# One written order for every step up to the second expert layer, in an attention and feed-forward kernel

## The chip, the core and the metric

The kernel runs on one core of a Trainium2 chip. The metric is the device time of one execution in microseconds (us); lower is better. The core has five engines with an instruction stream each: TensorE (PE) multiplies matrices into PSUM, VectorE (DVE) and ScalarE (ACT) do elementwise work and reductions, GpSimd (POOL) does small work here, and SyncE (SP) issues the transfers (DMA).

## What is computed

Inputs are `q`, `k`, `v` of 8 batches × 12 heads × 448 tokens × 64, and two weight matrices of 768×2048 and 2048×768, which the kernel reads as 64-bit numbers.

```python
scores = scale * q @ k.T - log(448);  attn = sigmoid(scores);  x = attn @ v
h = x @ w_in                                  # 3584 x 768 by 768 x 2048
g = where(h > 0, h, exp(min(h, 0)) - 1)
out = g @ w_out                               # 3584 x 2048 by 2048 x 768
```

There is no normalisation over keys: each score has its own sigmoid.

## The kernel before

The work goes batch by batch (b = 0 to 7), and within a batch by pairs of heads (`hp` = 0 to 5; 48 pairs in all). The first batch multiplies 32-bit numbers. Later ones split each 32-bit operand into a high and a low 16-bit part (`split`, L138: ACT makes the high part, L139, and DVE the low part, L140) and multiply three combinations of them, with scales that are powers of two.

A pair is **prepared**: greatest magnitudes on DVE (`absmax`, L143), summed over partitions on PE (`pr`, L131), made into scales on DVE and POOL; then for b=0 transposed on PE (`pt`, L362) and copied (`early`, L366), and for later batches split (`nat`) and transposed by a DMA (L377). Then come **scores** (`psc`, L408), **sigmoid** on ACT (`sg`, L416), for later pairs the split of the sigmoids (`at`, L454 and L455), **values** (`pav`, L480), and the split of the result into `xh` with its greatest magnitude.

When a batch's six pairs are there, `xh` is rescaled (L519 to L532), and the **first expert layer's product** follows (`moe1`, `ph`, L570: 16 tiles of 18 matmuls), with the exponential on ACT (L582), the rest of the nonlinearity on DVE (L584, L585) and the split into `g`. The **output product** of a batch (`moe2`, `po`, L602: 96 steps of 6 matmuls for an even batch) runs among the attention steps of the next batch.

The **weights** need work of their own, once. Each of the 16 tiles of `w_in` (768 KB) is loaded into a ring of five places (`load_w_in`), turned from 64-bit words into magnitudes by two ACT steps (L156, L160) and one DVE step (L161), summed on PE (`si`, L168), scaled, given its sign (L175), and split into `wi`. The 32 half tiles of `w_out` take the same path (`load_w_out`, `so`), but the scale of a half (`swo`) is there only once all 16 of its tiles have been summed.

What sets the order: from the attention of b=1 on, it is written out in the program (`tc.manual_schedule` holds PE, ACT, DVE and SP to program order). All before that, which is the attention and first layer of b=0 with all of `w_in` and most of `w_out`, is ordered by the framework's scheduler, which works with its own estimates of durations; the lists `W_IN`, `W_LOAD`, `W_OUT` and `W_AHEAD` only say beside which step a weight tile is written down. The staging area of `w_in` and the tile `wo` share one buffer (tag `wo`), as do `early` and `g` (tag `g`).

Of the kernel before, what the change touches and what calls it, by code (L numbers as in the profile page):

```python
# [32 lines left out]

@with_exitstack
def attention_ffn(
# [24 lines left out]
    WHOLE = EXACT * NP + 2  # L60
    SP = 4
    SKEW = 2
    W_IN = [1, 3, 6, 9, 12, 15, 16]
    W_LOAD = [1, 1]
    W_OUT = 4
    W_AHEAD = [6, 2]
# [12 lines left out]
    wi = const.tile([P, 2, NK, DF], F16, name="wi")  # L79

# [9 lines left out]
    stage, w_in_words = [], []  # L90
# [18 lines left out]
    def greatest(dst, mx):  # L109

        dg = sb.tile([P, P], BF16, tag="dg", name="dg")
        nc.vector.tensor_scalar(dg, ident, mx, None, op0=ALU.mult)

        def rest():
            pb = ps.tile([P, 512], F32, tag="pm", name="pb", bufs=3)
            nc.tensor.matmul(pb[:, :P], ones, dg, start=True, stop=True)
            al = sb.tile([P, 1], F32, tag="al", name="al", bufs=2)
            nc.vector.tensor_reduce(al, pb[:, :P], axis=AX.X, op=ALU.max)
            power_of_two(dst, al, XTINY)

        return rest

    def sums_of_rows(dst, mx, parts):

        n = mx.shape[1]

        def rest():
            pb = ps.tile([P, 512], F32, tag="pm", name="pr", bufs=3)
            sums = pb[:, : 4 * n].rearrange("p (n x) -> p n x", x=4)
            for r in parts:  # L130
                nc.tensor.matmul(sums[r], ones[:, r], mx, start=True, stop=True)  # L131
# [4 lines left out]
        return rest  # L136

    def split(hi, lo, src, s):  # L138
        nc.scalar.mul(hi, src, s)  # L139
        nc.vector.scalar_tensor_tensor(lo, src, s, hi, op0=ALU.mult, op1=ALU.subtract)  # L140
# [9 lines left out]
    def magnitudes(t, lo, hi, hl, sums, start, stop):  # L150


        u, h = t.bitcast(U32), hi.bitcast(F32)


        nc.scalar.activation(t, h, AF.Abs, scale=2.0**-112)  # L156


        top = hl.bitcast(U16).rearrange("p a (c t) -> p a c t", t=4)[:, :, :, 1]
        nc.scalar.activation(lo, top, AF.Copy, scale=2.0**-13, bias=2.0**-14 - 0.5)  # L160
        nc.vector.scalar_tensor_tensor(  # L161
            u, u, 3, lo, op0=ALU.logical_shift_left, op1=ALU.bitwise_or
        )

# [23 lines left out]
    def load_w_in(n):  # L188

        src = w_in.rearrange("(c p) f -> p c f", p=P)  # L190
        for _ in range(n):
            f = len(w_in_words)
            if f == 0:

                stage.append(sb.tile([P, WR * 2 + WT, NK * P], F32, tag="wo", name="stage"))
            if f < NF:
                st = stage[0][:, f % WR * 2 : f % WR * 2 + 2]
                st = st.rearrange("p a c -> p (a c)").rearrange("p (c x) -> p c x", c=NK)
                nc.sync.dma_start(st.bitcast(U64), src[:, :, f * P : (f + 1) * P])
                w_in_words.append(words(st))  # L200

    def w_in_tile(f):
        lo, hi, hl = w_in_words[f]
        t = stage[0][:, WR * 2 + f % WT].rearrange("p (c x) -> p c x", c=NK)
        sums = ps.tile([P, 512], F32, tag="pm", name=f"si{f}", bufs=3)
        magnitudes(t, lo, hi, hl, sums[:, :P], True, True)
        sum_magnitude(wp[:, f : f + 1], sums[:, :P])
        nc.vector.reciprocal(wr[:, f : f + 1], wp[:, f : f + 1])
        s = sb.tile([P, 1], F32, tag="sw", name=f"swi{f}", bufs=2)
        nc.gpsimd.tensor_scalar(s, wr[:, f : f + 1], 2.0**WTOP, None, op0=ALU.mult)  # L210
        d = wi[:, :, :, f * P : (f + 1) * P]
        signed(t, hi)
        split(d[:, 0], d[:, 1], t, s)

    def w_in_ratios():
# [4 lines left out]
    def load_w_out(wo):  # L220


        for i in range(NH):
            whole = [
                wo[:, i, f + SKEW].rearrange("p j c -> p (j c)").bitcast(F32)
                for f in range(NF - SKEW)
            ] + [
                sb.tile([P, HM], F32, tag="o", name=f"to{i}_{f}", bufs=OB) for f in range(SKEW)
            ]
            sums = ps.tile([P, 512], F32, tag="pav", name=f"so{i}")  # L230
            loads = []

            def load(f):
                if f >= NF:
                    return
# [14 lines left out]
                loads.append(st)  # L250

            early = W_AHEAD[i]
            for f in range(early):
                load(f)
            for f in range(NF):
                load(f + early)
                lo, hi, hl = words(loads[f])
                t = whole[f].unsqueeze(1)
                magnitudes(t, lo, hi, hl, sums[:, :HM], f == 0, f == NF - 1)
                signed(t, hi)  # L260
                yield
            sum_magnitude(wop[:, i : i + 1], sums[:, :HM])
# [3 lines left out]
            for f in range(NF):  # L266
                split(wo[:, i, f, 0], wo[:, i, f, 1], whole[f], s[:, 1 + f : 2 + f])
                yield


# [4 lines left out]
    def load_qk(b, hp):  # L275
# [3 lines left out]
        for i, src in enumerate((q, k)):  # L279
            for j in range(2):  # L280
                nc.sync.dma_start(  # L281
                    raw[:, i * (NC + 1) :][:, :NC, j],
                    src[b, h0 + j, :SM].rearrange("(p c) d -> p c d", c=NC),
                )
# [36 lines left out]
    def prepare(b, hp, raw, rv, xs):  # L321


        u = f"{b}_{hp}"
        n = 1 if b < EXACT else 3
        mx = sb.tile([P, 15], BF16, tag="mx", name=f"mx{u}", bufs=2)
        groups = mx.rearrange("p (n x) -> p n x", x=5)[:, :n, :4]
        absmax(mx[:, 0:4], rv.rearrange("p (a t) d -> p a (t d)", a=4))
        if n > 1:

            absmax(mx[:, 6 : 2 * NC + 7], raw.rearrange("p t h d -> p t (h d)"))
# [3 lines left out]
        pw = sb.tile([P, n], F32, tag="pw", name=f"pw{u}", bufs=2)  # L335
        apart = b >= EXACT and (hp > 2 or hp == (2 if b == EXACT else 0))
        product = sums_of_rows(pw, groups, rows if apart else [slice(0, P)])

        def scales():
            product()  # L340
            sc = sb.tile([P, n + 3], F32, tag="sc", name=f"sc{u}", bufs=5)
            if b >= EXACT:
# [10 lines left out]
            value_scale(b, hp, pw[:, 0:1], sc[:, n : n + 1], xs)  # L353
            return lambda: transposed(sc)

        def transposed(sc):
            x_scale, s_rest, s_scale = (sc[:, n + i : n + i + 1] for i in range(3))
            if b < EXACT:
                pt = ps.tile([P, 2, 512], F32, tag="psc", name=f"pt{u}", bufs=2)
                pt = pt.rearrange("p a x -> p (a x)")  # L360
                for t in range(2 * NC + 1):
                    nc.tensor.transpose(  # L362
                        pt[:, t * P : (t + 1) * P], raw[:, t].rearrange("p h d -> p (h d)"), ident
                    )
                qk = early[:, hp % 2]
                nc.vector.tensor_copy(qk, pt[:, : 2 * S])  # L366
                return x_scale, 1 / math.sqrt(D), [qk], [rv]
            nat = sb.tile([P, 2, 2 * NC + 1, P], F16, tag="nat", name=f"nat{u}")
            for t, n_t, s in (
                (0, NC, sc[:, 1:2]), (NC, 1, s_rest), (NC + 1, NC, sc[:, 2:3])  # L370
            ):
                split(
                    nat[:, 0, t : t + n_t], nat[:, 1, t : t + n_t],
                    raw[:, t : t + n_t].rearrange("p t h d -> p t (h d)"), s,
                )
            qk = sb.tile([P, 2, 2 * NC + 1, P], F16, tag="qk", name=f"qk{u}", bufs=3)
            nc.sync.dma_start_transpose(  # L377
                qk.rearrange("p i t x -> p (i t) x"), nat.rearrange("p i t x -> p (i t x)")
            )
            parts = [qk[:, i].rearrange("p t x -> p (t x)") for i in range(2)]  # L380

            if b * NP + hp < WHOLE:
                whole = sb.tile([P, 2 * NC + 2, D], F32, tag="vn", name=f"vw{u}", bufs=3)
                return x_scale, s_scale, parts, [load_v(b, hp, whole)]
            vn = sb.tile([P, 2, 2 * NC + 2, D], F16, tag="vn", name=f"vn{u}", bufs=3)
            split(vn[:, 0], vn[:, 1], rv, sc[:, 0:1])
            return x_scale, s_scale, parts, [vn[:, 0], vn[:, 1]]

        return scales

    class Pair:
# [42 lines left out]
        def parts(self, g):  # L434
# [435 lines left out]
```

## Time and profile before

| | us |
|---|---|
| median of three runs | 1201.78 (1201.6 to 1202.27) |
| the profiled execution | 1201.61 |
| its span, first to last instruction | 1199.8 |
| busy: PE, DVE, ACT, POOL | 1148.5, 817.2, 710.1, 95.9 |

A stage table gives the busy time of each engine within a stretch. A timeline row gives start, length, engine, line, operation, output and inputs, the number of instructions merged into it, and in brackets the idle time before it with what ended it. A row of groups gives count, busy us, mean ns of one, then the idle time before them. The letter q behind an engine means its queue (SPq: SyncE's issuing).

### The profile page before, as it was taken

How to read it: one execution, taken by the hardware profiler on the slowest of the kernel's cores; microseconds unless marked ns; L12 is line 12 of the kernel's file. 1: busy time of each engine (PE TensorE's matmuls, PEld its weight loads, DVE VectorE, ACT ScalarE, POOL GpSimd, SP SyncE). 2: the span in 40 equal slices, each digit the busy share in tenths (PEclk: the TensorE clock that was granted, in tenths of full speed). 3: DMA queues.
4: the chain of work that ended last, by engine and by line, in shares of the span. 5: the costliest groups of instructions: out<-in, count | busy, mean ns of one | idle time of the engine just before them, and what ended most of it. 6: DMA issues, size and time to landing. Idle time of an engine off the chain costs nothing.

```text
span 1199.8 us, 24004 instructions
## 1 busy us (share of the span) xinstructions
PE 1148.5 (96%) x9662; PEld 634.7 (53%) x9662; DVE 817.2 (68%) x1730; ACT 710.1 (59%) x1087; POOL 95.9 (8%) x275
## 2 busy tenths in 40 slices
PE   6779976999999999999999999999999999999998
PEld 2224433555566555555566555655566555655565
DVE  4798888877577575876677575976667666864500
ACT  4785796855566447864666446865666446864300
POOL 1011001100011001100011000200011000100000
PEclk9989988999999999999999999999999999999999
DMA  8874634521234130531224221441134212310000
GB/s 220 260 191 96 220 107 114 104 61 41 47 79 95 34 68 20 115 78 40 41 65 96 53 51 37 94 100 40 40 61 93 61 40 47 70 30 8 1 27 27
DMA packets 220687, 92.14 MB, mean 77 GB/s; under 512 B 184224, under 2 KB 216480, under 8 KB 220576
## 3 DMA queue, kind: packets, MB, share of 16 engines
q1 hardware_dynamic: 220576, 90.61, 31.3%
q8 instruction: 75, 1.23, 0.4%
q14 instruction: 36, 0.29, 0.1%
HBM read 60.29 MB, written 11.01 MB: 59 GB/s over the span
## 4 chain that ended last, share of the span: by engine, by line
PE 85%; DMA 5%; DVE 4%; ACT 3%; SPq 2%; issue 1%; DVEq 0%; POOL 0%; ACTq 0%; POOLq 0%
PE ph L570 32%; PE po L602 31%; PE pav L480 7%; PE psc L408 7%; PE po_r L602 5%; DMA stage<-in_moe_w_in_dram 3%; PE pscr L500 1%; DMA wo<-in_moe_w_out_dram 1%; SPq L281 1%; ACT sg L416 1%; DMA so<-in_moe_w_out_dram 1%; ACT wo L139 1%; DVE wo L175 1%; DVE wo L140 1%; DVE wi L140 1%
## 5 line engine op out<-in xcount | busy, mean ns | idle before, releaser
L570 PE MATMUL ph<-xh,wi 128*128 128x448 f16 x2304 | 441.7, 353 | 1.7 <-DVE e L585 0.9
L602 PE MATMUL po<-wo,g 128*64 128x384 f16 (+1 forms) x4320 | 395.7, 328 | 6.9 <-ACT wo L139 3.8
L602 PEld LDWEIGHTS <-g 128*64 128x64 f16 (+1 forms) x4992 | 290.3, 109 | 169.6 <-issue 40.4
L570 PEld LDWEIGHTS <-wi 128*128 128x128 f16 x2304 | 223.0, 98 | 214.3 <-issue 8.0
L582 ACT ACTIVATE e<-ph,msc 128x448 f32<-128x448 f32 x128 | 80.7, 631 | 185.8 <-PE ph L570 161.1
L455 DVE SCALAR_TENSOR_TENSOR at<-sg,at 128x896 f16<-128x896 f32 x120 | 127.6, 1091 | 92.2 <-ACT at L454 92.2
L416 ACT ACTIVATE sg<-psc,bias,sc 128x896 f32<-128x896 f32 x126 | 133.5, 1094 | 3.6
L584 DVE TENSOR_SCALAR e<-e 128x448 f32<-128x448 f32 x128 | 50.2, 393 | 117.1 <-ACT e L582 117.1
L454 ACT ACTIVATE at<-sg 128x896 f16<-128x896 f32 x120 | 109.4, 947 | 0.6
L139 ACT ACTIVATE g<-e,msc 128x384 f16<-128x384 f32 (+1 forms) x192 | 96.1, 533 | 11.3 <-DVE e L585 9.9
L139 ACT ACTIVATE xh<-pav,sc 128x448 f16<-128x448 f32 x48 | 30.3, 631 | 119.8 <-PE pav L480 117.3
L140 DVE SCALAR_TENSOR_TENSOR g<-e,msc,g 128x384 f16<-128x384 f32 (+1 forms) x192 | 94.8, 522 | 1.9 <-ACT g L139 1.5
L585 DVE SCALAR_TENSOR_TENSOR e<-ph,msc,e 128x448 f32<-128x448 f32 x128 | 87.5, 684 | 4.1
L408 PE MATMUL psc<-qk 64*128 64x448 f16 x756 | 86.5, 352 | 2.2 <-ACT sg L416 2.2
L480 PE MATMUL pav<-at,vn 128*64 128x448 f16 x720 | 74.8, 353 | 0.0
L139 ACT ACTIVATE nat<-raw,sc 128x384 f16<-128x384 f32 (+1 forms) x126 | 60.7, 535 | 10.2 <-POOL sc L347 8.4
L480 PEld LDWEIGHTS <-vn 128*64 128x64 f16 x880 | 49.9, 110 | 31.2
L349 POOL TENSOR_SCALAR sc<-pw 128x1 f32<-128x1 f32 x42 | 12.2, 292 | 662.7 <-DVE pw L105 563.8
L602 PE MATMUL po_r<-wo,g 128*64 128x384 f16 (+1 forms) x672 | 64.9, 327 | 0.0
L140 DVE SCALAR_TENSOR_TENSOR nat<-raw,sc,nat 128x384 f16<-128x384 f32 (+1 forms) x126 | 60.6, 526 | 3.9 <-ACT nat L139 1.8
L140 DVE SCALAR_TENSOR_TENSOR xh<-pav,sc,xh 128x448 f16<-128x448 f32 x48 | 32.6, 680 | 37.1 <-ACT xh L139 37.1
L610 DVE TENSOR_SCALAR o<-po,osc 128x384 f32<-128x384 f32 x48 | 29.4, 612 | 41.1 <-PE po L602 36.4
(112 smaller groups left out, 928.5 us busy)
## 6 DMA issues: line engine op xcount, KB each, us to landing
stage<-in_moe_w_in_dram SPq DMA_DIRECT2D x16, 768.0 KB, 6.6
raw<-in_q_dram SPq DMA_DIRECT2D x96, 96.0 KB, 3.3
raw<-in_k_dram SPq DMA_DIRECT2D x96, 96.0 KB, 2.9
rv<-in_v_dram SPq DMA_DIRECT2D x48, 192.0 KB, 2.8
out_dram<-o SPq DMA_DIRECT2D x48, 192.0 KB, 2.1
wo<-in_moe_w_out_dram SPq DMA_DIRECT2D x19, 384.0 KB, 3.8
so<-in_moe_w_out_dram SPq DMA_DIRECT2D x13, 384.0 KB, 3.7
rv<-in_v_dram SPq DMA_DIRECT2D x96, 32.0 KB, 2.5
```

The lines of the kernel that those rows point to most:

```text
L139: nc.scalar.mul(hi, src, s)
L140: nc.vector.scalar_tensor_tensor(lo, src, s, hi, op0=ALU.mult, op1=ALU.subtract)
L408: nc.tensor.matmul(psc[:, j, :S] if g < NC else psc[rows[j], 0, :S], kk[rows[j], o], qq[rows[j], :S], start=(n == 0), stop=(n == len(parts ...
L416: a = nc.scalar.activation(to, psc, AF.Sigmoid, bias=bias, scale=self.s_scale)
L454: nc.scalar.mul(hi, sg, 2.0**ATOP)
L455: nc.vector.scalar_tensor_tensor(lo, sg, 2.0**ATOP, hi, op0=ALU.mult, op1=ALU.subtract)
L480: nc.tensor.matmul(pav[rows[j], :S], vv[i][:, 2 * NC + j if g == NC else j * NC + g], sg[k][:, j], start=(g == 0 and n == 0), stop=(g == N ...
L570: nc.tensor.matmul(ph[:, :S], wi[:, wj, c, f * P : (f + 1) * P], xh[:, c, xj], start=(n == 0), stop=(n == 3 * NK - 1),)
L582: a = nc.scalar.activation(e, ph[:, :S], AF.Exp, scale=inv)
L584: nc.vector.tensor_scalar(e, e, 1.0, -1.0, op0=ALU.min, op1=ALU.add)
L585: nc.vector.scalar_tensor_tensor(e, ph[:, :S], inv, e, op0=ALU.mult, op1=ALU.max)
L602: nc.tensor.matmul(po[r, :HM], tokens[:, r], wo[:, i, f, wj], start=(n == 0), stop=(n == 3 * NF - 1),)
```

## The change

The work up to the second expert layer (the one of b=1) is cut into forty generators, called streams, of steps that use one engine each. A string `ORDER` of 969 letters says which stream takes its next step. All of it now stands within `manual_schedule`, so PE, ACT, DVE and SP each run their steps as the string has them.

Steps that were one function are divided for it: `prepare` becomes the class `Preparation`, `moe1` the class `Expert`, `split` its ACT half and its DVE half, `w_in_tile` seven streams, `load_w_out` eight, `finish` three. From the second expert layer on, the loop puts the same steps in the same order as before.

Two things beside: the two loads for the two heads of `q` (and of `k`) become one DMA each, and `wo` and `g` have fixed places, in which the `w_in` staging and `early` lie as views.

```diff
+ORDER = (
+    "iqviiqviiAAAAAABaCbdEDceBCDESSBFTaCGSbWFTATAAAdWWSDEceBGCEDBiiqTSWvFAAXTSCSGBTAFTSTYDEYa"
+    "GWCiiqAAAFAbWWWdEDcXvieiqBGABYBaSCSTTSTFWACbSdWWEcDATFeEGGSWSCivTXATAAYDBYDaSSCWbWBcETAF"
+    "FdeGioqoiTAACWWSSvEDBBiEqiGDYFTTXSSTCAAFTGYaCdbEceWWWWSSGDEBDAAXABARBTFTCCSCSEEGETFDHHFH"
+    "YHTYRGovqWWWWvDGDFHHFXRYRGGYYRaRRIoooooooHHHHHHHHHHRIaRJJrRIIKKIIabmJJJJmKKKKIIcJHHxKyIx"
+    "HHofHHooooJKoyIIHHHHHHmxHHzHHIIIomJJJJJJKGyKfHxHmzxKzIKKKJKoomHgyIyIJLKgaHzMMHxHNwwooumJ"
+    "mMHHxzfxIywJNKyKIHHMNIgNImJbmMwNyKzMoqoxHzzxHMNHHMJJmyKycNIwKNwtovuoxfMmxHfNJgHMMwIyNwzw"
+    "NgMKIyNmHHfxMzzzJmgwyxIKwyoHHzaIJmmqotoMxxzywKNJJKNKzMHyzHawwIHMHoHHvINwNIwppppppppppppb"
+    "ppSSJJJppppppppppppppTTSppKKKcafoooHHffHHHHgaIIIJJJLgTSSTMMNMNNMMkWWpWpbpppppppppppppppp"
+    "NNMMNNMMgNMNKMNKNMNKfgMTMNMTNcMNjtqvkWXfffSSTfTYgggaappppppppWbWWWgctqjvffffgggNgqSSTXpp"
+    "pppppYkYYaUVTUVaSSTTUVvjtpppWpTUpSSTTkabcUfffaVggVgWppppSSppWppWpppTUUUfXVVVSpppYgYkTTST"
+    "tSTTjqvjbWWWSSpWppppUUUXURRRRcVVYVaVpWpWWWTTUUSpppppppTXUUfffaVVYYVVRYkRRWWWWXfYYggggqvj"
+    "t"
+)
...
-    W_IN = [1, 3, 6, 9, 12, 15, 16]
-    W_LOAD = [1, 1]
-    W_OUT = 4
-    W_AHEAD = [6, 2]
+    wo = const.tile([P, NH, NF, 2, HM], F16, name="wo")
+    g = const.tile([P, 2, NF, SM + 2 * R], F16, name="g")
+    stage = wo.rearrange("p i f j c -> p (i f j c)").bitcast(F32)
+    stage = stage.rearrange("p (r x) -> p r x", x=NK * P)[:, NF - 2 * WR - WT :]
+    early = g[:, 1, NF - 7 :].rearrange("p f s -> p (f s)").bitcast(F32)
...
-            for j in range(2):
-                nc.sync.dma_start(
-                    raw[:, i * (NC + 1) :][:, :NC, j],
-                    src[b, h0 + j, :SM].rearrange("(p c) d -> p c d", c=NC),
-                )
+            nc.sync.dma_start(
+                raw[:, i * (NC + 1) :][:, :NC],
+                src[b, h0 : h0 + 2, :SM].rearrange("h (p c) d -> p c h d", c=NC),
+            )
...
+    def w_in_fields():
+        for f in range(NF):
+            lo, hi, hl = w_in_words[f]
+            field(staged(f), hi)
+            yield
+            last_bits(lo, hl)
+            yield
...
+    streams = {
+        "q": qk_loads(), "v": v_loads(), "i": load_w_in(), "o": load_w_out(),
+        "t": pair_turned(), "u": whole_values(), "j": outputs(),
+        "A": w_in_fields(), "B": w_in_magnitudes(), "C": w_in_add(), "D": w_in_scales(),
+        "E": w_in_signs(), "F": w_in_high(), "G": w_in_low(),
+        "H": w_out_fields(), "I": w_out_magnitudes(), "J": w_out_add(), "K": w_out_signs(),
+        "L": w_out_scales(), "M": w_out_high(), "N": w_out_low(),
+        "a": maxima(), "b": maxima_sums(), "c": pair_scales(), "d": pair_transposes(),
+        "e": pair_copies(), "f": pair_high(), "g": pair_low(),
+        "S": scores(), "T": sigmoids(), "U": sigmoids_high(), "V": sigmoids_low(),
+        "W": value_products(), "X": x_high(), "Y": x_low(),
+        "R": rescaled(), "r": greatest_product(),
+        "m": first_layer("products"), "x": first_layer("exponential"),
+        "y": first_layer("elu"), "z": first_layer("high"), "w": first_layer("low"),
+        "p": output_products(), "k": evictions(),
+    }
...
     with tc.manual_schedule(engines={E.PE, E.Activation, E.DVE, E.SP}):
-        for b in range(EXACT, B):
-            out_scale(*of_moe2, slice(0, 1 if b == EXACT else NH))
-            tiles = moe2(b - 1, g, wo)
+        for c in ORDER:
+            next(streams[c])
```

On DVE are the streams B, D, E, G, I, K, L, N, V, Y, a, c, e, g, R, y, w and k; on PE C, J, S, W, b, d, r, m and p; on ACT A, F, H, M, T, U, X, f, x and z; on SP the rest. The first `m` is the 332nd letter, the first `p` the 604th.

More of the change, by code (lines that the diff above doesn't have):

```diff
@@ L186, in sum_magnitude, with staged, load_w_in @@
         )
-    def load_w_in(n):
+    def staged(f):
+        return stage[:, WR * 2 + f % WT].rearrange("p (c x) -> p c x", c=NK)
+    def load_w_in():
         src = w_in.rearrange("(c p) f -> p c f", p=P)
[L191 to L213, printed above, removed]
@@ L218, in w_in_ratios, with load_w_out @@
         nc.gpsimd.tensor_scalar(wn, wp, wm[:, 1:2], 2.0**WTOP, op0=ALU.mult, op1=ALU.mult)
-    def load_w_out(wo):
+        yield
+    w_out_words, w_out_whole, w_out_sums, w_out_scale = {}, {}, {}, {}
+    def load_w_out():
         for i in range(NH):
[L224 to L235, printed above, removed]
+            for f in range(NF):
                 if i == 0 and f >= 2:
@@ L334, in prepare, with sums, scales @@
             )
[L335 to L342, printed above, removed]
+        def sums(self):
+            b, hp = self.b, self.hp
+            apart = not self.exact and (hp > 2 or hp == (2 if b == EXACT else 0))
+            groups = self.mx.rearrange("p (n x) -> p n x", x=5)[:, : self.groups, :4]
+            self.reach = sums_of_rows(groups, rows if apart else [slice(0, P)])
+        def scales(self):
+            n = self.groups
+            pw = sb.tile([P, n], F32, tag="pw", name=f"pw{self.u}", bufs=2)
+            self.reach(pw)
+            sc = sb.tile([P, n + 3], F32, tag="sc", name=f"sc{self.u}", bufs=5)
+            if not self.exact:
                 nc.vector.reciprocal(sc[:, :n], pw)
@@ new lines, in scales, with transposes @@
+            if self.hp == 0:
+                xs_of[self.b] = sb.tile([P, 3, NP], F32, tag="xs", name=f"xs{self.b}", bufs=2)
+            value_scale(self.b, self.hp, pw[:, 0:1], sc[:, n : n + 1], xs_of[self.b])
+            self.sc = sc
+            self.x_scale, self.s_rest, self.s_scale = (
+                sc[:, n + i : n + i + 1] for i in range(3)
+            )
+        def transposes(self):
+            pt = ps.tile([P, 2, 512], F32, tag="psc", name=f"pt{self.u}", bufs=2)
+            self.pt = pt.rearrange("p a x -> p (a x)")
+            for t in range(2 * NC + 1):
+                nc.tensor.transpose(
+                    self.pt[:, t * P : (t + 1) * P],
+                    self.raw[:, t].rearrange("p h d -> p (h d)"), ident,
+                )
@@ L385, in transposed, with split @@
[L385 to L389, printed above, removed]
+            vs = [self.whole] if self.n < WHOLE else [self.vn[:, 0], self.vn[:, 1]]
+            ready[self.n] = self.x_scale, self.s_scale, parts, vs
+        def split(self):
+            for i in range(3):
+                self.natural(i)()
+            if self.n >= WHOLE:
+                self.values()()
+            self.transposed()
@@ L546, in moe_scales, with __init__, products @@
         nc.vector.tensor_scalar(m[:, 1], m[:, 1], xr, None, op0=ALU.mult)
[L550 to L559 removed]
+    class Expert:
+        def __init__(self, b, xh, m):
+            self.b, self.xh, self.m = b, xh, m
+            self.runs = [(0, 0, S)] if b % 2 == 0 else [(0, 0, SM), (SM, SM + R, R)]
+            self.ph, self.e = {}, {}
+        def products(self, f):
+            b = self.b
             if f == 3 and b >= EXACT:
@@ L707, in hidden @@
-    def hidden(b, beside=None):
-        xh, xs = xh_of.pop(b), xs_of.pop(b)
-        whole = rescale(b, xh, xs)
-        next(whole)
-        yield
-        xp, xr, rest = next(whole)
-        m = sb.tile([P, 2, NF], F32, tag="msc", name=f"msc{b}")
-        def first():
-            rest()
-            moe_scales(m, xs, xr)
-        moe1(b, g, xh, m, first, beside)
-        yield b, xs, xp
+    begun, of_pair, preparation = {}, {}, {}
+    later = []
+    def pair_of(n):
+        if n not in of_pair:
+            b, hp = pairs[n]
+            if hp == 0:
+                xh_of[b] = []
+                if b == EXACT and K:
+                    ahead = sb.tile([P, K, 2, S], F16, tag="xa", name="xa")
+                    xh_of[b] += [ahead[:, c] for c in range(K)]
+            if len(xh_of[b]) == hp:
+                here = sb.tile([P, NK, 2, S], F16, tag="xh", name=f"xh{b}")
+                xh_of[b] += [here[:, c] for c in range(hp, NK)]
+            of_pair[n] = Pair(b, hp, *ready.pop(n), xh_of[b], xs_of[b])
+        return of_pair[n]
@@ new lines, in qk_loads, with v_loads, maxima, maxima_sums @@
+    def qk_loads():
+        for n in range(AHEAD + 2):
+            raws[n] = load_qk(*pairs[n])
+            yield
+    def v_loads():
+        for n in range(AHEAD + 2):
+            loaded[n] = raws.pop(n), load_v(*pairs[n])
+            yield
+    def maxima():
+        for n in range(AHEAD + 1):
+            p = begin(n)
+            p.greatest()
+            yield
+            if not p.exact:
+                p.greatest_qk()
+                yield
+    def maxima_sums():
+        for n in range(AHEAD):
+            preparation[n].sums()
+            yield
@@ new lines, in pair_scales, with pair_transposes, pair_copies, pair_high @@
+    def pair_scales():
+        for n in range(AHEAD):
+            preparation[n].scales()
+            yield
+    def pair_transposes():
+        for n in range(FIRST):
+            preparation[n].transposes()
+            yield
+    def pair_copies():
+        for n in range(FIRST):
+            preparation[n].copied()
+            yield
+    naturals = []
+    def pair_high():
+        for n in range(FIRST, AHEAD):
+            for i in range(3):
+                naturals.append(preparation[n].natural(i))
+                yield
+            if n >= WHOLE:
+                naturals.append(preparation[n].values())
+                yield
@@ new lines, in sigmoids, with sigmoids_high, sigmoids_low, value_products @@
+    def sigmoids():
+        while True:
+            softens.pop(0)()
+            yield
+    sigmoid_parts = []
+    def sigmoids_high():
+        for n in range(WHOLE, LAST):
+            for t in range(NC + 1):
+                sigmoid_parts.append(of_pair[n].high(t))
+                yield
+    def sigmoids_low():
+        while True:
+            sigmoid_parts.pop(0)()
+            yield
+    def value_products():
+        for n in range(LAST):
+            for t in range(NC + 1):
+                of_pair[n].values(t)
+                yield
@@ new lines, in x_high, with x_low, layer, first @@
+    def x_high():
+        for n in range(LAST):
+            of_pair[n].finish_high()
+            yield
+    def x_low():
+        for n in range(LAST):
+            of_pair[n].finish_low()
+            yield
+            of_pair[n].finish_most()
+            yield
+    def layer(b):
+        xh, xs = xh_of.pop(b), xs_of.pop(b)
+        whole = rescale(b, xh, xs)
+        for _ in range(NP + 1):
+            next(whole)
+            yield
+        next(whole)
+        yield
+        xp, xr, last = next(whole)
+        m = sb.tile([P, 2, NF], F32, tag="msc", name=f"msc{b}")
+        def first():
+            reciprocal = last()
+            def rest():
+                reciprocal()
+                moe_scales(m, xs, xr)
+            return rest
+        yield Expert(b, xh, m), first, (b, xs, xp)
@@ new lines, in attention_ffn, with rescaled, greatest_product, first_layer @@
+    layers, firsts = {}, {}
+    def rescaled():
+        l = layers[0] = layer(0)
+        for _ in range(NP + 2):
+            next(l)
+            yield
+        layers[0], first, begun[0] = next(l)
+        firsts[0] = first
+        yield
+        firsts[1]()
+        yield
+        l = layers[1] = layer(1)
+        for _ in range(NP + 1):
+            next(l)
+            yield
+    def greatest_product():
+        firsts[1] = firsts[0]()
+        yield
+    def first_layer(step):
+        def run():
+            for f in range(NF):
+                getattr(layers[0], step)(f)
+                yield
+        return run()
@@ new lines, in output_products, with evictions, outputs @@
+    def output_products():
+        yield from moe2(0, later)
+    sends = []
+    def evictions():
+        for n in range(NH * NC):
+            if n % NC == 0:
+                out_scale(*begun[0], slice(n // NC, n // NC + 1))
+            sends.append(later.pop(0)())
+            yield
+    def outputs():
+        for n in range(NH * NC):
+            sends.pop(0)()
+            yield
+    streams = {
[14 more added lines that the diff above has]
+    }
@@ L769, in beside @@
+    prepared = AHEAD
     def beside(f):
-        nonlocal third
+        nonlocal prepared
+        p = preparation.get(prepared)
+        if p is None:
+            return
         if f in (2, 8):
-            third = scales()
+            p.sums()
+            p.scales()
         if f in (4, 10):
-            third()
-            prepare_next()
-    third = None
+            p.split()
+            load_pair(prepared + 2)
+            prepared += 1
+            if prepared < len(pairs):
+                begin(prepared).greatest()
+                preparation[prepared].greatest_qk()
@@ L820, in attention_ffn @@
                 if works:
-                    third()
-                    prepare_next()
-                if b == EXACT and hp < NC:
-                    step(3 if hp < NC - 1 else NF)
+                    preparation[prepared].split()
+                    load_pair(prepared + 2)
+                    prepared += 1
+                    if prepared < len(pairs):
+                        begin(prepared).greatest()
+                        preparation[prepared].greatest_qk()
                 if hp == NP - 1:
-                    h = hidden(b, beside if b + 1 < B else None)
-                    next(h)
+                    l = layer(b)
+                    for _ in range(NP + 1):
+                        next(l)
                 fill(share - gap - tail)
```

514 lines of the change are left out of this document (302 added, 212 removed).

## The prediction

> **What bounds the kernel now.** I read the stages first. The second expert layer (`ph`, L570, for b=1) starts at 257.0 us, so the table cuts the span there, at the first `ph` of b=0 (91.3) and at the first `po` (156.2), with the worst stretch of the last part beside it. Columns: stretch, its length, then busy us and records for PE, PEld, DVE, ACT, POOL, then granted clock, DMA share, GB/s.
>
> ```profile
> 0.00:91.30 91.30, 64.59 (x338) 25.40 (x339) 66.01 (x163) 62.13 (x79) 8.35 (x28) 0.94 0.82 222
> 91.30:156.20 64.90, 60.86 (x326) 30.37 (x322) 56.91 (x141) 42.88 (x82) 5.58 (x18) 1.00 0.50 151
> 156.20:257.00 100.80, 84.44 (x851) 45.62 (x851) 85.26 (x175) 80.38 (x126) 11.40 (x32) 0.93 0.45 109
> 160.00:200.00 40.00, 24.42 (x177) 10.39 (x178) 34.01 (x74) 33.13 (x60) 4.73 (x11) 0.83 0.41 113
> 0.00:257.00 257.00, 209.88 (x1510) 101.39 (x1511) 208.17 (x475) 185.39 (x286) 25.33 (x77) 0.95 0.60 159
> 257.00:1199.80 942.80, 938.59 (x8155) 533.35 (x8153) 609.06 (x1256) 524.73 (x801) 70.57 (x198) 1.00 0.24 54
> ```
>
> The reader should see two kernels in one. From 257.0 on PE works 938.6 of 942.8 us at full clock: nothing but less PE work shortens that, and the change leaves its matmuls, copies and order alone there (the loop for b≥2 issues what it issued). Everything at stake lies in the first 257.0 us, where no engine is full: DVE 208.2, ACT 185.4. From 160 to 200 PE works 24.4 of 40 us; the page's row of `po` names the output weights `wo` as what it waited for:
>
> ```profile
> L602 PE MATMUL po<-wo,g 128*64 128x384 f16 (+1 forms) x4320 | 395.7, 328 | 6.9 <-ACT wo L139 3.8
> ```
>
> **The change, part by part.** The same steps stand before the second expert layer as before (counted from the string: 96 output steps, 16 of the first layer, 13 pairs prepared, all 16 and 32 weight tiles). So the question is how far the idle time shrinks, and I build the new 257.0 from three stages that the string itself cuts: up to the first `m` (first layer's products), up to the first `p` (output products), and the rest.
>
> *Start.* The weight load now stands first on SP's queue; before, it stood behind the nine loads of a pair.
>
> ```profile
> 0.72 1.34 SPq L281 DMA_DIRECT2D raw<-in_q_dram  x2
> ...
> 6.74 0.59 SPq L199 DMA_DIRECT2D stage<-in_moe_w_in_dram  x1
> ```
> ```profile
> 13.95 0.96 DVE L161 SCALAR_TENSOR_TENSOR stage<-stage 128x768 uint32<-128x768 uint32 x1 [4.25 <-ACT stage L160]
> ```
>
> From issue (6.74) to the first weight step on DVE took 7.2 us; issued at 0.72 it is there at **7.9**, and DVE, which does almost nothing before, starts 6 us earlier. What is queued behind: six ACT weight steps precede the first sigmoid, and they need the third weight tile, which stands behind nine issues of some 0.65 us (1.34 for two above): issued at 6.6, with the same 7.2 its second step is done at 13.8, and the sigmoid comes then. PE waits for it, with nothing to lose that early. Joining the two loads per head of `q` and of `k` takes two of nine issues of 0.67 from each pair; SP is behind for no one after this, PE is full later, so zero; if one joined issue takes as long as two, also zero. Fixed places for `wo` and `g` only let output-weight loads start as soon as their own slot is free; they are counted at nothing, being hidden behind the DVE work below.
>
> *Up to the first `m`.* Ahead of it the string has on DVE 16 each of B, E, D and G, 6 copies of `pt`, 12 Y, 8 maxima of `rv`, and some ten us of small ones.
>
> ```profile
> L140 DVE SCALAR_TENSOR_TENSOR wi<-stage,swi,wi 128x768 f16<-128x768 f32 x16 | 16.0, 1011 | 2.8 <-ACT wi L139 2.8
> L161 DVE SCALAR_TENSOR_TENSOR stage<-stage 128x768 uint32<-128x768 uint32 x16 | 15.2, 950 | 8.5 <-ACT stage L160 8.5
> L175 DVE SCALAR_TENSOR_TENSOR stage<-stage 128x768 uint32<-128x768 uint32 x16 | 15.2, 949 | 0.0
> ...
> L143 DVE TENSOR_REDUCE mx<-rv 128x4 bf16<-128x512 f32 x14 | 9.4, 680 | 2.8 <-DMA rv<-in_v_dram 2.8
> ...
> L140 DVE SCALAR_TENSOR_TENSOR xh<-pav,sc,xh 128x448 f16<-128x448 f32 x12 | 8.1, 675 | 0.7 <-ACT xh L139 0.7
> L143 DVE TENSOR_REDUCE xs<-xh 128x1 f32<-128x448 f16 x12 | 7.3, 609 | 0.0
> L366 DVE COPY early<-pt 128x896 f32<-128x896 f32 x6 | 6.5, 1086 | 8.2 <-PE pt L362 8.2
> ...
> L182 DVE TENSOR_REDUCE alw<-si 128x1 f32<-128x128 f32 x16 | 4.5, 281 | 2.0 <-PE si L168 2.0
> ```
> ```profile
> 42.53 0.95 DVE L161 SCALAR_TENSOR_TENSOR stage<-stage 128x768 uint32<-128x768 uint32 x1
> 43.40 0.15 DVE L104 TENSOR_SCALAR al<-al 128x1 f32<-128x1 f32 x1
> ```
>
> Records overlap: steps of 0.95 follow each other at 0.87, so each counts 0.08 less. B and E 32×0.87=27.8, G 16×0.93=14.9, D 16×(0.20+3×0.07)=6.5, Y 6×(0.60+0.53)=6.7, copies 6×1.01=6.0, maxima 8×0.60=4.8; the rest (eight output-weight steps at half a B each, ten rescaling steps, six pairs' scales, one maximum of `raw`) some 10, an estimate from the same rows. Sum **77 us**. PE has less there, so DVE sets the pace:
>
> ```profile
> 62.07 0.51 PE L168 MATMUL si<-stage,ones 128*128 128x128 bf16 x6
> 62.51 0.97 PE L480 MATMUL pav<-sg,rv 128*64 128x448 f32 x4
> 63.41 0.99 PE L362 MATMUL pt<-ident,raw 128*128 128x128 f32 x7
> 64.33 0.97 PE L468 MATMUL pav<-sg,rv 64*64 64x448 f32 x4
> ...
> 85.84 1.76 PE L480 MATMUL pav<-sg,rv 128*64 128x448 f32 x4 [5.26 <-DVE xh L140]
> ```
>
> Start to start, a step of scores or values is 0.90, a transposing step 0.92, a weight sum 0.44: 48×0.90+6×0.92+16×0.44=55.8. DVE's idle time after its start cannot be read for an order not yet run; its bounds are zero and what the old order left there, 91.3−7.9−(66.0−0.4)=17.8. I take half, **9**: half because the rows above split it so, 8.5 behind ACT's weight steps (whose loads now come 6 us earlier and further ahead) and 8.2 behind transposes, which the joined loads hardly hasten. First `m` at 7.9+77+9=93.9. PE has then just waited for the rescaling: the last row above shows the same four matmuls at 1.76 after a wait of 5.26, against 0.97; I add **1**, with bounds 0 and 2: 94.9.
>
> [...]
>
> *First `m` to first `p`.* PE has 16×18 products and 24 sums of output weights, each as long as one pair of half-tile products (4.90/30=0.16, below).
>
> ```profile
> 204.59 2.42 PE L480 MATMUL pav<-sg,vw 128*64 128x448 f32 x12
> 206.95 0.97 PE L468 MATMUL pav<-sgr,vw 64*64 64x448 f32 x4
> ...
> 211.68 0.74 PE L408 MATMUL psc<-qk 64*128 64x448 f16 x6
> 212.35 0.76 PE L500 MATMUL pscr<-qk 64*64 64x448 f16 x12
> 213.04 5.07 PE L602 MATMUL po<-wo,g 128*64 128x384 f16 x60
> 217.94 1.87 PE L480 MATMUL pav<-at,vn 128*64 128x448 f16 x18
> 219.64 0.55 PE L480 MATMUL pav<-ar,vn 128*64 128x448 f16 x4
> ...
> 267.30 20.59 PE L570 MATMUL ph<-xh,wi 128*128 128x448 f16 x108
> ```
>
> 288×20.59/108=54.9, with the sums **58.9**. Idle: bounds zero and the old stage's 64.9−60.9=4; taken **2**. First `p` at 155.8. This is no earlier than before (156.2); the difference is that all 16 weight tiles of the first half stand ahead of it in the string, so the waits for `wo` fall away for 48 of the 96 steps.
>
> *First `p` on.* PE has 576 half-tile products (4.90 for 60, start to start: 47.0), 6 sums (1.0), 18 score groups of 0.67 and 3 of 0.69 (14.1), two pairs of values at 2.36+0.90 (6.5), four at 1.70+0.48 (8.7): **77.4**. From the first `m` on PE thus has 136.3 us and DVE 208.2−77=131, ACT less: PE sets the pace, narrowly. Idle on PE: zero at best; at worst what the old order lost between 160 and 200, 15.6. I take **4**, nearer zero, because that loss came from the unfinished weights, and the second half's quantisation now runs beside 30 `p` steps of the first half. End of the part: 155.8+77.4+4=**237.2** instead of 257.0, a gain of 19.8. The profiled execution took 1201.61, 1.8 outside its span of 1199.8, and the median is 1201.78: it becomes **1182.0**.
>
> **The rivals.** *The idle time before the first `p` stays* (17.8 and 4): the waits are handoffs of four engines in line, which no order removes. First `p` at 166.6, end at 248.0, time 1192.8. For it: DVE's waits above end with ACT and PE, not with DMA. Against: there is other work to put in them.
>
> *The last part stalls*, the slower side: with every engine strictly in order, a `p` stands on PE behind values, these behind DVE's and ACT's halves of the sigmoids, and those behind each other; DVE has 63 of its 131 us (estimate: half) in this part and cannot run ahead. If PE stays at the 24.42/40=61% of 160 to 200, 77.4 take 126.9: end at 282.7, time 1227.5. It decides once PE falls below 77.4/(257.0−155.8)=76% there. Against: from 200 on the old order, with the same steps on PE, DVE and ACT, had none of it.
>
> *PE cold in the first stage*: each wait long enough slows what follows, as in the row with 1.76 for 0.97. All 55.8 us at (1.76−0.07)/0.90=1.88 are 105 and pass DVE's 86: first `m` 19 us later, time 1201, no change. Against: the old granted clock there was 0.94. [...]
>
> *The order does not take hold* (another engine's free order or the transfers undo it) and only the early weight load counts: 6 us, time 1195.8. Against it: all five queues but POOL's are listed, and POOL has 25 of 257 us.
>
> **How the numbers follow.** Forecast 0.70, with its own range 1172 to 1191 (the stalls of 15 in the sum doubled, or cut by two thirds); idle before `p` stays 0.12; last part stalls 0.10; cold PE 0.04; does not take hold 0.04. With no stall anywhere the end is at 7.9+77+58.9+77.4=221.2, time 1166; with every upper bound at once 7.9+77+17.8+2+58.9+4+77.4+15.6=260.6, time 1205.4. Two such extremes together are unlikely; the range is 1168 to 1200, leaving out 0.03 below and some 0.13 above. A measurement here tells 0.2% (2.4 us) from no change. Faster: forecast 0.70, first rival 0.12, last 0.04 = 0.86; the cold case is the same, 0.04; slower 0.10.
>
> **What would show it.** First weight step on DVE near 8 us; first `ph` near 95 with DVE over 88% busy from 8 us on; first `po` near 156 and no stretch of 20 us after it with PE under 17 busy; `ph` of b=1 near 237; from there 943 us to the end. The forecast is wrong if that last length changes, if the first `ph` comes after 105, or if PE waits more than 12 us between the first `po` and the second layer's `ph`.

## The result and the profile after

The changed kernel takes **1182.55 us** (median of 4 runs, 1182.28 to 1182.78), the kernel before 1201.93 beside it: a ratio of 0.9839, 95% interval 0.9822 to 0.9856. Predicted were 1182.0, in a range of 1168 to 1200. (The streams, counted, are 44, not forty.)

The stage table of the changed kernel, cut at the same three events: the first `ph` of b=0 (92.81), the first `po` (156.08) and the first `ph` of b=1 (236.06). Columns as in the table of before.

```profile
0.00:92.81 92.81, 63.54 (x340) 26.53 (x341) 79.96 (x184) 68.85 (x90) 11.37 (x30) 0.95 0.83 226
92.81:156.08 63.27, 61.77 (x314) 30.93 (x313) 58.98 (x136) 47.13 (x93) 5.46 (x15) 0.96 0.57 164
156.08:236.06 79.98, 78.81 (x858) 45.74 (x857) 72.50 (x150) 68.06 (x103) 10.17 (x32) 1.00 0.46 106
160.00:200.00 40.00, 38.93 (x410) 22.82 (x406) 34.30 (x81) 31.54 (x53) 6.22 (x21) 1.00 0.47 109
236.06:1180.50 944.44, 938.75 (x8154) 533.42 (x8153) 612.76 (x1264) 526.03 (x803) 70.59 (x198) 1.00 0.25 55
```

The first event comes 1.5 us later than before (91.3), the second where it stood (156.2). All of the gain shows in the third row: 80.0 us from the first `po` to the second layer instead of 100.8. DVE's work was moved ahead for it: the first row has 80.0 us of it instead of 66.0, the third 72.5 instead of 85.3. From 160 to 200 PE now works 38.9 of 40 us, before 24.4. The last row is 1.6 us longer than before. The page's row for `po` shows that its 6.9 us of waiting are gone:

```profile
L778 PE MATMUL po<-wo,g 128*64 128x384 f16 (+1 forms) x4320 | 392.4, 327 | 0.0
```

Two places show what is left. These are PE's timeline rows around the first layer of b=0, and of b=1:

```profile
90.73 0.46 PE L197 MATMUL so<-wo,ones 128*128 128x384 bf16 x1 [4.95 <-DVE wo L188]
...
92.81 5.93 PE L715 MATMUL ph<-xh,wi 128*128 128x448 f16 x18
...
99.26 3.57 PE L715 MATMUL ph<-xh,wi 128*128 128x448 f16 x18
...
241.05 0.22 PE L136 MATMUL pb<-dg,ones 128*128 128x128 bf16 x1 [1.42 <-DVE dg L132]
```

After a wait of 4.95 us the first 18 products take 5.93 us, the next 18 take 3.57. The granted clock (the third number from the right) was 0.50 in the first of these stretches and 1.00 in the second:

```profile
92.81:97.00 4.19, 4.19 (x13) 1.75 (x13) 4.05 (x14) 3.31 (x8) 0.00 (x0) 0.50 0.84 332
98.00:102.00 4.00, 4.00 (x23) 2.14 (x22) 3.02 (x8) 1.78 (x2) 0.00 (x0) 1.00 0.36 90
```

And after the first products of b=1, PE waits 1.42 us for `dg`, which DVE makes behind four steps of a later pair's preparation (`nat` three times, `vn`). These are DVE's rows, and below them those of the kernel before, where no such steps stand between the greatest magnitude of `xh` (`xs`) and `dg`:

```profile
238.54 1.40 DVE L163 SCALAR_TENSOR_TENSOR nat<-raw,sc,nat 128x384 f16<-128x384 f32 x3
239.86 0.75 DVE L163 SCALAR_TENSOR_TENSOR vn<-rv,sc,vn 128x512 f16<-128x512 f32 x1
...
240.71 0.29 DVE L132 TENSOR_SCALAR dg<-ident,rr 128x128 bf16<-128x128 f32 x1
```
```profile
256.83 0.61 DVE L143 TENSOR_REDUCE xs<-xh 128x1 f32<-128x448 f16 x1
257.35 0.60 DVE L610 TENSOR_SCALAR o<-po,osc 128x384 f32<-128x384 f32 x1
257.88 0.15 DVE L527 TENSOR_REDUCE rr<-xs 128x1 f32<-128x6 f32 x1
258.06 0.29 DVE L112 TENSOR_SCALAR dg<-ident,rr 128x128 bf16<-128x128 f32 x1
```

### The profile page after: what moved, and what is told of

It reads as the page before. It is cut to its first block, busy times and chain, and to the rows that moved or that the text cites. A ratio compares the mean times of both kernels' runs of the same rounds, so it can differ in the third digit from the quotient of the medians.

```text
span 1180.5 us, 23847 instructions
## 1 busy us (share of the span) xinstructions
PE 1142.9 (97%) x9662; PEld 636.6 (54%) x9662; DVE 824.2 (70%) x1730; ACT 710.1 (60%) x1087; POOL 97.6 (8%) x275
## 3 DMA queue, kind: packets, MB, share of 16 engines
q8 instruction: 75, 1.23, 0.4%
## 4 chain that ended last, share of the span: by engine, by line
PE 85%; DVE 11%; ACT 1%; issue 1%; DMA 1%; SPq 0%; POOL 0%; DVEq 0%; POOLq 0%; ACTq 0%
PE ph L715 33%; PE po L778 30%; PE psc L529 7%; PE pav L608 7%; PE po_r L778 5%; DVE wo L204 1%; DVE wo L163 1%; PE pscr L638 1%; DVE wo L188 1%; DVE wi L163 1%; DVE g L163 1%; DVE e L733 1%; DVE mx L170 1%; DVE at L163 1%; DVE nat L163 0%
## 5 line engine op out<-in xcount | busy, mean ns | idle before, releaser
L481 ACT ACTIVATE nat<-raw,sc 128x384 f16<-128x384 f32 (+1 forms) x126 | 60.9, 534 | 13.3 <-POOL sc L445 7.8
L163 DVE SCALAR_TENSOR_TENSOR nat<-raw,sc,nat 128x384 f16<-128x384 f32 (+1 forms) x126 | 60.9, 526 | 3.5 <-ACT nat L481 1.6
```

Of the source, the lines that this page charges most:

```text
L481: nc.scalar.mul(self.nat[:, 0, t : t + n], src, s)
```

## The experiments

### The weight load behind the first pair

```diff
-ORDER = "iqviiqvii" ...
+ORDER = "qviiqviii" ...
```

> Only the order on SP's queue changes: the first weight tile is asked for behind the loads of the first pair, two more right behind it, and the rest as in the changed kernel. Theory A (before the first ph, DVE's work is the path, and whatever starts it later ends it later): the first weight step on DVE moves from 7.3 to about 12 us, the first ph from 92.8 to about 97, and the time from 1182.5 to 1186 to 1188. Theory B (the stage has slack between ACT and PE, the early load is taken up by it): first ph within 1 us of 92.8, time 1182 to 1184.

Only one weight tile, not two, is asked for right behind the first tile here; the third now stands behind the second pair's loads, so it moves too.

Measured: 1185.64 us, ratio to before 0.9864 (0.985 to 0.9879). The rows are DVE's and PE's, of this run; in the changed kernel the same DVE step started at 7.25.

```profile
12.57 0.96 DVE L188 SCALAR_TENSOR_TENSOR wo<-wo 128x768 uint32<-128x768 uint32 x1 [11.35 <-ACT wo L184]
...
96.61 4.70 PE L715 MATMUL ph<-xh,wi 128*128 128x448 f16 x18
```

DVE starts 5.3 us later, the first `ph` comes 3.8 us later, the end 3.1 later. From DVE's first weight step to the first `ph` are 84.0 us (12.57 to 96.61), in the changed kernel 85.6, of which DVE is busy for 79.7. So the stage is bound by DVE's work from its first step, and only 1.5 of 5.3 us are absorbed. The end loses less than the first `ph` does; those 18 products took 4.70 us instead of 5.93. Theory A holds, with a median just below its numbers.

### The same string, ordered by the framework

```diff
-    with tc.manual_schedule(engines={E.PE, E.Activation, E.DVE, E.SP}):
-        for c in ORDER:
-            next(streams[c])
+    for c in ORDER:
+        next(streams[c])
+    with tc.manual_schedule(engines={E.PE, E.Activation, E.DVE, E.SP}):
```

> The same steps, written down in the same sequence, but the string's part stands outside the fixed schedule, so the framework orders PE, ACT, DVE and SP with its own estimates of durations, as it did in the kernel before. Theory A (the gain is the order that the engines keep to): most of the gain goes, 1195 to 1203, with PE idle again after the first po. Theory B (the gain is in the finer steps, the fixed places and the sequence as written, whoever orders them): 1180 to 1187.

Measured: 1205.47 us (median of ten runs, 1201.39 to 1208.38), ratio 1.0028 (1.0017 to 1.0039): the whole gain is gone, and a little more, past theory A's numbers. The finer steps, the fixed places, the joined loads and the sequence as written are all still there. PE's timeline shows the first `ph`, two waits after the first `po` (161.1 in this run), and the start of the second layer:

```profile
90.40 5.26 PE L715 MATMUL ph<-xh,wi 128*128 128x448 f16 x18 [2.37 <-DVE xh L659]
...
186.29 4.17 PE L608 MATMUL pav<-sg,vw 128*64 128x448 f32 x12 [4.54 <-DVE alw L211]
...
244.81 1.30 PE L529 MATMUL psc<-qk 64*128 64x448 f16 x6 [6.42 <-ACT sgr L537]
...
255.47 2.44 PE L715 MATMUL ph<-xh,wi 128*128 128x448 f16 x12
```

Up to the first `ph` the framework's order is no worse: it comes at 90.4, 2.4 us ahead of the changed kernel. The second layer starts 19.4 us later than there. DVE had done 69.9 us of work by the first `ph`, not 80.0. So what keeping to the order is worth lies almost all between these two events.

### Plain program order, kept to

```diff
-ORDER = <the string up to the first m> + ...
+ORDER = <per weight tile AABCDEFG, then the next load; per pair abcde, four times STW, XYY> + <the rest of that part> + ...
```

> The letters up to the first m are put in plain program order, weight tile by weight tile and pair by pair (the sequence in which the kernel before wrote them down, with weight loads four tiles ahead), then all that is left of that part; the rest of the string is unchanged. Theory A (keeping to an order is worth nothing by itself, the interleaving is what fills DVE): DVE waits out the chain ACT, DVE, PE, DVE, POOL, ACT of each tile, the first ph comes at 120 us or later, and the time is above 1205. Theory B (finer steps held to program order are enough): first ph within 6 us of 92.8, time below 1189.

Measured: 1317.79 us, ratio 1.0944 (1.0906 to 1.0982). The stage up to the first `ph` of this run, and four of the longest waits of DVE, ACT and PE in its first 240 us (columns: total us, times, longest):

```profile
0.00:228.56 228.56, 96.12 (x341) 34.98 (x341) 85.05 (x184) 71.60 (x91) 14.57 (x30) 0.62 0.34 92
```
```profile
DVE xh L163 <- ACT xh L615: 85.5, 6, 18.0
ACT sg L537 <- PE psc L529: 78.3, 22, 5.4
...
PE si L197 <- DVE wo L188: 70.5, 16, 5.4
ACT wi L267 <- POOL swi L256: 64.8, 16, 9.0
```

The first `ph` comes at 228.6 instead of 92.8, with the same 184 DVE steps in 85 us of busy time. Each engine stands behind a step that waits for another one's, and PE's granted clock falls to 0.62, so that its 340 matmuls are busy for 96 us instead of 64. How much of the 136 us is the chain of handoffs and how much is the slow PE within that chain, this run does not separate. Together with the run before it says: neither the sequence without keeping to it, nor keeping to a sequence as such, gives anything.

### The 30 covering output steps put later

```diff
-... wNIwppppppppppppbppSSJJJppppppppppppppTTSppKKKcafoooHHffHHHHgaIIIJJJLgTSSTMMNMNNMMk ...
+... wNIwbSSJJJTTSKKKcafoooHHffHHHHgaIIIJJJLgTSSTMMNMNNMMppppppppppppppppppppppppppppppk ...
```

> The 30 output steps that stand before the second half of the output weights has been summed are put behind those sums (in front of the first eviction); nothing else moves. Theory A (after the first po PE sets the pace, and these 30 steps are what it does while the second half is prepared): PE has little to do for 10 to 15 us there, the 30 x 0.49 = 14.7 us come later, and the time is 1192 to 1198. Theory B (DVE and ACT set the pace in the last part, PE has room): 1182 to 1186.

Measured: 1195.94 us, ratio 0.9948 (0.9934 to 0.9963), 13.4 above the changed kernel; the 30 steps are 14.7 us of PE. The stage in which they were missing, and the one after it:

```profile
154.30:175.00 20.70, 8.29 (x45) 2.45 (x44) 17.74 (x41) 15.58 (x27) 2.52 (x10) 0.71 0.41 124
175.00:247.00 72.00, 71.98 (x792) 41.94 (x792) 52.30 (x104) 50.54 (x74) 6.91 (x23) 0.99 0.35 81
```

PE works 8.3 of 20.7 us while DVE and ACT prepare the second half, and then 72.0 of 72.0. So PE is the path of the last part, and those steps are its cover. Theory A.

### The early load alone, in the kernel before

```diff
-    for n in range(2):
-        load_pair(n)
-        load_w_in(W_LOAD[n])
+    load_w_in(1)
+    load_pair(0)
+    load_pair(1)
+    load_w_in(1)
```

> The kernel before, with one thing of the change alone: the first weight tile is asked for ahead of the loads of the first two pairs, the second right behind them; the framework orders the rest as it did. Theory A (an early start is only worth what the order makes of it; the old order's waits for the output weights after the first po stay): first weight step on DVE near 7 us, time 1198 to 1203. Theory B (the rival in the prediction: the early load alone is worth its 6 us): 1194 to 1197.

Measured: 1207.04 us, ratio 1.0044 (1.003 to 1.0058), slower than before and outside both theories' numbers. The first weight step on DVE starts at 7.3, as wanted, but the framework's order then has the old waits, some of them longer:

```profile
7.32 0.96 DVE L161 SCALAR_TENSOR_TENSOR stage<-stage 128x768 uint32<-128x768 uint32 x1 [6.11 <-ACT stage L160]
...
92.08 0.67 PE L168 MATMUL si<-stage,ones 128*128 128x128 bf16 x6 [4.61 <-DVE stage L161]
94.89 8.46 PE L570 MATMUL ph<-xh,wi 128*128 128x448 f16 x33 [2.12 <-DVE xh L521]
...
170.05 0.35 PE L602 MATMUL po<-wo,g 128*64 128x384 f16 x2 [3.79 <-ACT wo L139]
...
186.88 0.48 PE L168 MATMUL so<-wo,ones 128*128 128x384 bf16 x1 [5.27 <-DVE wo L161]
...
262.45 3.58 PE L570 MATMUL ph<-xh,wi 128*128 128x448 f16 x18
```

The first `ph` comes 3.6 us later than before, the second layer at 262.45 instead of 257.0. An early start is worth 3 us in the written order and less than nothing in the other. Why the framework's order came out worse, these runs do not show.

### PE kept busy before the first products

```diff
+    def kept_busy():
+        pk = ps.tile([P, 512], F32, tag="pm", name="pk", bufs=3)
+        for _ in range(22):
+            nc.tensor.matmul(pk[:, :S], wi[:, 0, 0, :P], wi[:, 0, 0, :S], start=True, stop=True)
+        yield
-ORDER = ... "RRIoooooooHHHHHHHHHHRIaR" + "JJrRIIKKIIabm" ...
+ORDER = ... "RRIoooooooHHHHHHHHHHRIaR" + "n" + "JJrRIIKKIIabm" ...
...
-        "p": output_products(), "k": evictions(),
+        "p": output_products(), "k": evictions(), "n": kept_busy(),
```

> The changed kernel, with 22 products of weights that nobody reads put on PE while it waits for the rescaling before the first ph (some 4.2 us of work in the 4.9 us wait from 85.7 to 90.7). Theory A (the first ph took 5.93 us instead of 3.57 because PE's clock had dropped in that wait, and PE is the path from there on): first ph 3.5 to 3.8 us long, time 1179.5 to 1181.0. Theory B (DVE is the path in that stage and catches up, or the first ph was slow because it waits for something): ph as long as before or time within 0.7 of 1182.5.

Measured: 1179.9 us (1179.66 to 1180.18), ratio 0.9818 (0.9805 to 0.9832), 2.65 below the changed kernel. PE's timeline:

```profile
85.52 4.33 PE L1033 MATMUL pk<-wi 128*128 128x448 f16 x22
...
92.47 3.57 PE L715 MATMUL ph<-xh,wi 128*128 128x448 f16 x18
```

The first `ph` takes 3.57 us instead of 5.93, with a granted clock of 1.00 over it, and starts 0.3 us earlier; the end comes 2.65 earlier. Theory A: the slow products were PE's clock, and PE is the path from there on.

### `dg` first, and both together

```diff
-        for c in ORDER:
+        for c in ORDER[:-8]:
             next(streams[c])
         b, l = EXACT, layers[EXACT]
+        next(l)
+        for c in ORDER[-8:]:
+            next(streams[c])
```

The last eight letters, `ggggqvjt`, are thus issued behind the step that makes `dg`; the loop's own first `next(l)` falls away. The second kernel has this, the products of the run before, and the first `m` in front of the `b` that preceded it.

> The changed kernel, with the greatest magnitude and the diagonal dg of the second layer put on DVE ahead of the last four low halves of a pair's preparation (they stood behind them, and PE waited 1.42 us for dg after the first ph of b=1). Theory A (PE is the path there): the 1.42 us go, 1180.7 to 1181.6. Theory B (the wait is made up later, by the exponentials or otherwise): within 0.5 of 1182.5.

> The products of the run before last and the early dg together, and the first ph put ahead of the sum of magnitudes (the letter b) that stands before it and waits 0.6 us for DVE. Theory A: the gains add, 2.2+1.4+0.5, so 1177.8 to 1179.8. Theory B: less than half of it, above 1180.5.

Measured: `dg` first 1180.05 us (1179.25 to 1181.55), 2.5 lower in the median, 0.65 past theory A's numbers, with runs that spread more than those of the changed kernel; all three **1177.77 us** (1177.39 to 1177.95), ratio 0.98 (0.9787 to 0.9814), at the lower edge of theory A's. In the profile of the kernel with `dg` first, and then in that of the combined one, `pb` follows the first products of b=1 without the wait:

```profile
236.95 3.58 PE L715 MATMUL ph<-xh,wi 128*128 128x448 f16 x18
240.36 0.22 PE L136 MATMUL pb<-dg,ones 128*128 128x128 bf16 x1
```

```profile
90.83 3.57 PE L715 MATMUL ph<-xh,wi 128*128 128x448 f16 x18
...
233.13 3.58 PE L715 MATMUL ph<-xh,wi 128*128 128x448 f16 x18
236.55 0.22 PE L136 MATMUL pb<-dg,ones 128*128 128x128 bf16 x1
```

From the second layer's start to the end are 1179.8−236.95=942.85 and 1176.0−233.13=942.9 us, as in the kernel before (942.8), where the changed kernel has 944.4. So 1.6 us of the gain are the `dg`; what its own run showed beyond that lies within its spread. The combined kernel's first layer starts 2 us earlier than the changed kernel's, at full speed, but of the start that the earlier `m` gains only some 0.6 us is left at the second layer (233.13, against 233.69 with the products alone). This version is faster than both kernels.

### The loads of two heads apart again

```diff
-            nc.sync.dma_start(
-                raw[:, i * (NC + 1) :][:, :NC],
-                src[b, h0 : h0 + 2, :SM].rearrange("h (p c) d -> p c h d", c=NC),
-            )
+            for j in range(2):
+                nc.sync.dma_start(
+                    raw[:, i * (NC + 1) :][:, :NC, j],
+                    src[b, h0 + j, :SM].rearrange("(p c) d -> p c d", c=NC),
+                )
```

> The changed kernel with the loads of the two heads of q, and of k, as two DMAs each again (two more issues of 0.6 to 0.7 us on SP per pair, in the string's part and after it). Theory A (SP's queue is behind for no one, or for the first tiles alone): 1181.5 to 1184.5. Theory B (the string asks SP for loads so densely in its first 65 us that 10 issues of 1.3 us more come late to ACT and DVE): first ph 3 us later or more, time above 1185.5.

Measured: 1184.77 us (1183.96 to 1185.32), ratio 0.9857 (0.9841 to 0.9874), 2.2 above the changed kernel and just past theory A. But theory B is wrong too: the first `ph` comes at 93.3, half a microsecond later, which is less than profiles of the same order differ by (92.81 in the changed kernel, 92.14 in the one with `dg` first), and the first `po` at 155.7. The loss is one wait of PE in the last part, for a transposing DMA on SP's queue. PE's row, then SP's, of this run, and last SP's row for the same transpose in the changed kernel:

```profile
213.63 0.74 PE L530 MATMUL psc<-qk 64*128 64x448 f16 x6 [2.52 <-DMA qk<-nat]
```
```profile
201.58 1.23 SPq L368 DMA_DIRECT2D raw<-in_q_dram  x2
...
208.15 2.04 SPq L498 DMA_TRANSPOSE qk<-nat  x1
```
```profile
206.64 1.80 SPq L497 DMA_TRANSPOSE qk<-nat  x1
```

SP issues the transpose 1.5 us later. Two pairs' loads stand in front of it in the string, each with two issues more here. From its issue to the end of PE's wait for it are 5.5 us (208.15 to 213.63); in the changed kernel it landed 4.5 us after its issue. Why it took longer here, this run does not show.

## Why the prediction was right

**Start.** Put at 7.9 us, measured 7.25. It is worth 3.1 us at the end by the run with the late load, and only in the written order: put into the kernel before, it made that slower, so the rival "only the early load counts, 6 us" has no run on its side. The first sigmoid, put at 13.8, came at 17.0; what that costs, no run shows.

**Up to the first `m`.** The sum had 77 us of DVE work and 9 of idle time, together 86; it was 79.7 and 5.9:

```profile
7.25:92.81 85.56, 63.54 (x340) 26.43 (x340) 79.67 (x180) 65.71 (x86) 10.66 (x23) 0.95 0.83 229
```

The errors cancel, and that is luck. The work was put too low above all because the dense spacing of 0.08 less per step, read from two long steps, does not hold for the short steps of a tile's scale (at 26.33 in the changed kernel one of 0.15 is followed by the next 0.19 later): those of the 16 tiles were put at 6.5 us, and their records are 12.1, in four rows of which these are the first two:

```profile
L211 DVE TENSOR_REDUCE alw<-si 128x1 f32<-128x128 f32 x16 | 4.5, 283 | 0.9 <-PE si L197 0.9
L212 DVE TENSOR_SCALAR alw<-alw 128x1 f32<-128x1 f32 x16 | 2.5, 154 | 0.6
```

The idle time was too high because its bound and the reason for halving it misread the rows of before. Of the 17.8 us, 4.4 lie ahead of the first weight step (6.05 of length, 1.68 busy) and go with the early start by itself; 13.3 lie behind it:

```profile
7.90:13.95 6.05, 3.56 (x10) 1.29 (x9) 1.68 (x2) 1.68 (x3) 0.00 (x0) 1.00 1.01 241
13.95:91.30 77.35, 59.15 (x322) 22.89 (x323) 64.03 (x157) 58.96 (x75) 7.64 (x21) 0.93 0.85 234
```

And of the two groups by which it was halved, 4.25 of the 8.5 us behind ACT's weight steps are the wait before the first of them, and 6.80 of the 8.2 behind `pt` are the kernel's very start:

```profile
8.02 1.09 DVE L366 COPY early<-pt 128x896 f32<-128x896 f32 x1 [6.80 <-PE pt L362]
```

Later waits were thus 4.3 and 1.4 us. In the changed kernel they are 0.2 (6.2, of which 6.0 are the start) and 0.7:

```profile
L188 DVE SCALAR_TENSOR_TENSOR wo<-wo 128x768 uint32<-128x768 uint32 x16 | 15.1, 951 | 6.2 <-ACT wo L184 6.2
L470 DVE COPY g<-pt 128x896 f32<-128x896 f32 x6 | 6.5, 1084 | 0.7 <-PE pt L463 0.6
```

The **cold step** was put at 1 us; it is 5.93−3.57=2.36, and the run without it was 2.65 faster. The 1 was read from four matmuls at 1.76 instead of 0.97 behind a wait of 5.26; the granted clock over them (before, 85.80 to 87.20) was 0.50, and so it was over the products here. Only those four were counted; in the changed kernel the clock was 0.50 from 92.81 to 97.50, over 13 products, and 2.36 us lost are 4.7 us at half rate. Nor is the price fixed: after waits of 4.94 and 4.95 us (the run with `dg` first, the changed kernel) the 18 products took 5.93 us, after 4.81 (the loads apart) 5.01, after 4.76 (the late load) 4.70. What sets it between these, no run shows.

**First `m` to first `po`.** 58.9 us of products and sums and 2 of idle gave 60.9; measured 63.3, of which 2.4 is that cold step, counted ahead of this part in the sum. The first `po` came at 156.1 against 155.8.

**From the first `po`.** 77.4 us of work and 4 of idle, 81.4; measured 80.0 with PE busy for 78.8. That PE sets the pace there, and that 30 output steps cover the second half's preparation, is shown by the run that took the cover away (+13.4). The slower rival, a last part at 61% of PE, is what this order avoids; misplaced steps bring a stretch like it: 30 steps elsewhere left PE 40% busy for 20.7 us.

**What was wrong.** Two edits were put at nothing that cost or gave something. Of the rest the prediction says that "the change leaves its matmuls, copies and order alone there", so 942.8 us. It took 944.4, because the string ends with four DVE steps that the old order did not have in front of `dg` (so the order is not the same as before at that seam); what was not counted is what is moved ahead on DVE's queue there. A change of that length was one of the prediction's own signs of being wrong, and it came true by 1.6 us. And the joined loads: "SP is behind for no one after this, PE is full later, so zero" is wrong by 2.2 us; a transposing DMA stands behind them in SP's order, and PE, being full, has no slack to wait for it. These two nearly cancel as well. In the ranges, the forecast's own upper end of 1191 is not what its words say: stalls of 15 us doubled give 1197. The measured time lies well inside either.

The rivals. *Idle before the first `p` stays*: no; on DVE 5.9 us are left of 13.3 behind its first weight step, and on PE 1.5 of 4 from the first `ph` to the first `po`. *The order does not take hold*: no; without it the time is 1205.5. *PE cold in the first stage*: not in this order (granted clock 0.95 up to the first `ph`, PE busy for 63.5 us); in the plain order the granted clock there was 0.62, with PE busy for 96.1.

## What to carry to other kernels

Where several engines are each some 70 to 85% busy in a stage and none is full (PE, DVE and ACT were at 68 to 85% in the first and third part before), count each engine's work up to the events that the next stage needs; the largest of these sums, plus a few microseconds, is what the written order reached here: each of the three parts ended 3 to 9 us beyond the sum on record. An order has to be found and kept to: the same steps in plain sequence cost 136 us more up to the first layer, and found but left to the framework's estimates they gave nothing. At the seams of a written order look at what stands in front of a single short step that a full engine waits for (`dg`, a transposing DMA), and try giving PE something to do in a wait of some microseconds (4.95 here, worth 2.65) that ends in its own critical work.

## What had not been expected of the hardware

Twenty-two products that nobody reads, 4.33 us of PE time, made the kernel 2.65 us faster: behind a wait of 4.95 us the granted clock was 0.50 for 4.7 us (92.81 to 97.50), and that cost 2.36 us of a full engine's time. In the plain order, with PE busy for 42% of 228.6 us (96.1), the granted clock was 0.62 over the whole stretch. How much of that length the slow clock made, no run here separates. And a joined load of two heads (192 KB) took SP 0.62 us to issue in its shortest rows, and each of the two halves took as long (1.23 us for two, at 201.58 above). In the median of 48 a joined load took 0.62 us for `k` and 1.10 for `q`; one head's load in the kernel before took 0.62 and 0.63 (of 96), so that joining halved SP's time for `k` and saved 0.16 of 1.26 us for `q`.

```profile
2.73 0.62 SPq L367 DMA_DIRECT2D raw<-in_k_dram  x1
```
